# Swapping PSUM bank pairs, reordering steps and moving one input load in the prologue of a fused attention-and-MLP kernel

## The chip, the cores and the metric

The kernel runs on one core of one Trainium2 chip. The metric is the device time of one execution in microseconds (us); every run time quoted is a median of several executions. "Trace" and "profile" mean one execution recorded by the hardware profiler; a time inside an execution comes from one trace. Kernels are compared only within the same rounds.

## The reference, cut to what matters

```python
xn = layernorm(x)                                   # x: 2048 tokens x 448, in 16 tiles of 128 tokens
out = x + A(xn) + B(xn)
# A: linear attention, 16 heads of 28; q and k go through w_phi, then softmax(+) and softmax(-)
qkv = xn @ wqkv
phi_k = concat(softmax(k @ w_phi), softmax(-k @ w_phi));  kv = phi_k^T v;  ... ;  o @ wo
# B: mixer MLP
h  = gelu(layernorm(xn) @ w1);  h = shift_tokens(h) @ w2;  x1 = xn + h
     x1 + gelu(layernorm(x1) @ w3) @ w4
```

This is about the first 32 us. In that prologue the 16 tiles of x are loaded, normalised and transposed, V and the gelu of w1 are computed, and w_phi is folded into the q and k weights.

## The kernel before

PSUM, the memory that the matmuls here write their results to, is used as four pairs of banks, 0 to 3. To drain a pair is to copy its results out, which frees it for the next step. A step that goes to TensorE names its pair, and one instruction can drain both banks of a pair: V of tiles 2 and 3, 128x896, is drained by one ScalarE instruction of 0.91 us in the trace of this kernel. The program gives every engine its own list, and the traces show ScalarE's drains in the order of that list: tile 4's copy, V of tiles 2 and 3 and tile 5's copy, listed so, start at 12.07, 12.56 and 13.36 us here. A recorder derives the semaphore waits from which bytes and banks an instruction reads and writes, so choosing another pair changes who waits for whom without any other edit.

The names in the order list are these:

- `xn_T(i, b, n)` transposes n normalised tiles through pair b; ScalarE (or DVE) copies them to `xnT`.
- `V(i, k)` is half k of v for tiles i and i+1; `v_out(i, b)` drains it.
- `WA(g, k)` is w1's first two chunks of 128 columns for group g (four tiles), called "w1's first chunk" below; `wa_out` is its gelu.
- `WC(g, k)` is w1's third chunk for group g; `wc_out` is its gelu. `WD` is the fourth chunk.
- `spin(n, w)` issues n dummy matmuls that keep TensorE busy; `tables` is a table load on ScalarE (1.28 us in the trace).
- `FO(t, m, k)` folds w_phi into wk (t = 1) or wq (t = 0). DVE casts the results.

```python
load_x(0, 1)
load_x(1, 1, "ACT")
load_x(2, 1)
load_lap(wv, A_wqkv[:, 896:1344], ("ACT", "SP"))    # two halves of 224 KB, one on each queue
load_x(3, 1, "ACT")
load_x(4, 2)
...
def ln1_two(i):                                     # tiles 0,1 and 2,3
    for j in (i, i + 1):
        ln_stats(st, mv, xtok, j)                                        # DVE
        R.act(rs[:, j, 1:2], mv[:, j, 1:2], ACT.Sqrt, bias=epsb[:, 0:1]) # ScalarE
    for j in (i, i + 1):
        R.ew(dve, "reciprocal", rs[:, j, 0:1], rs[:, j, 1:2])
        ln1_apply(dve, j)
...
vps = {i: v_pair(i, b) for i, b in ((0, 2), (2, 3), (4, 1), (6, 3), (8, 1), (10, 1), (14, 3))}
was = {g: wa_pair(g, b) for g, b in ((0, 0), (1, 0), (2, 0), (3, 2))}
wcs = {g: wc_pair(g, b) for g, b in ((0, 2), (1, 2), (2, 0), (3, 3))}
...
play([(spin, 4, 256), V(0, 0), (xn_T, 2, 0), V(0, 1), (xn_T, 3, 1),
      (spin, 2, 256), V(2, 0), (v_out, 0, 2), (tables, "gelu_apprx_tanh_and_others"), WA(0, 0), (xn_T, 4, 1),
      V(2, 1), (v_out, 2, 3), (xn_T, 5, 2), WA(0, 1), WC(0, 0), (xn_T, 6, 3), WC(0, 1), (wc_out, 0, 2),
      V(4, 0), (xn_T, 7, 3), (wa_out, 0, 0), V(4, 1), (v_out, 4, 1), V(6, 0),
      ...
```

After the prologue come eight rounds of a k pair, a q pair and a side job, then the w3 and w4 stage to the end.

The softmax here doesn't subtract the row's maximum and nothing guards it: scores larger than these inputs give would overflow.

Of the kernel before, what the change touches and what calls it, by code (L numbers as in the profile page):

```python
# [5 lines left out]
ACT = mybir.ActivationFunctionType  # L6
# [214 lines left out]
def bass_parallel_sum__linear_kernel_hedgehog__mixer_s_mlp__prompt_kernel(  # L221
# [14 lines left out]
    with es:  # L236
# [18 lines left out]
        for b in range(4):  # L255
            t = es.enter_context(nc.psum_tensor("bank%d%d" % (2 * b, 2 * b + 1), [128, 1024], F32))
# [87 lines left out]
        def load_x(i, n, eng="SP"):  # L344
            R.dma(xtok[:, i:i + n, :], x2d[128 * i:128 * (i + n), :].rearrange("(j p) d -> p j d", p=128), eng)
# [5 lines left out]
        def load_lap(dst, src, engs=("SP", "SP")):  # L351
            for h in range(2):
                R.dma(dst[:, 2 * h:2 * h + 2, :], src[192 * h:192 * h + 256, :].rearrange("(c p) d -> p c d", p=128), engs[h])

        load_x(0, 1)
        load_x(1, 1, "ACT")
        load_x(2, 1)
        load_lap(wv, A_wqkv[:, 896:1344], ("ACT", "SP"))
        load_x(3, 1, "ACT")
        load_x(4, 2)  # L360
        load_x(6, 2)
        load_lap(w1, B_w1)
# [102 lines left out]
        def fold_pair(t, m, b):  # L465
            def side(k, hi):
                r, c0, c1 = (slice(64, CR), 2 * DH, CR) if hi else (slice(0, 64), 0, 3 * DH)
                return [(banks[2 * b + k][:, CR * c + c0:CR * c + c1],
                         wT[r, t, c, START[m + k]:START[m + k] + 128], bd[r, CR * c + c0:CR * c + c1])
                        for c in range(NC)]  # L470

            def late():
                row_pairs(side(1, 0), side(0, 1))
                if t:
                    R.ew(dve, "tensor_copy", wpk[:, m:m + 2, :], two(2 * b)[:, :, 0:D])
                    return
                for k in range(2):
                    a = banks[2 * b + k]
                    for j in range(2):
                        R.ew(dve, "tensor_copy",  # L480
                             wpq[:, m + k, :].rearrange("p (c j h e) -> p c j h e", c=NC, j=2, h=2)[:, :, j, :, 0:DH],
                             a[:, 224 * j:224 * j + 224].rearrange("p (c h e) -> p c h e", c=NC, h=2))
            return lambda: row_pairs(side(0, 0), side(1, 1), True), late
# [26 lines left out]
        def two(b):  # L510
            return pairs[b // 2].rearrange("p (b e) -> p b e", b=2)
# [3 lines left out]
        def row_pairs(first, second, start=False, cols=1):  # L515
            for s, (p, q) in enumerate(zip(first, second)):
                for out, lhs, rhs in (p, q) if cols == 1 else (*p, *q):
                    R.mm(out, lhs, rhs, start and s == 0, False)

        def lap_pair(outs, lhs, rhs):  # L520
            def side(k, rows, kcs):
                return [(outs[k], lhs(k, kc, *rows), rhs(k, kc, *rows)) for kc in kcs]
            return (lambda: row_pairs(side(0, LO, (0, 1, 2, 3)), side(1, HI, (0, 1, 2, 3)), True),
                    lambda: row_pairs(side(1, LO, (0, 1, 3)), side(0, HI, (0, 2, 3))))
# [11 lines left out]
        def v_pair(i, b):  # L536
            return lap_pair([banks[2 * b + k][:, 0:D] for k in range(2)],
                            lambda k, kc, lo, hi: xnT[lo:hi, kc, 128 * (i + k):128 * (i + k) + 128],
                            lambda k, kc, lo, hi: wv[lo:hi, kc, :])
# [9 lines left out]
        def wa_pair(g, b):  # L549
            return lap_pair([banks[2 * b + k] for k in range(2)],  # L550
                            lambda k, kc, lo, hi: w1[lo:hi, kc, 128 * k:128 * k + 128],
                            lambda k, kc, lo, hi: xnT[lo:hi, kc, 512 * g:512 * g + 512])
# [4 lines left out]
        def wc_pair(g, b):  # L557
            return lap_pair([banks[2 * b + k][:, 0:256] for k in range(2)],
                            lambda k, kc, lo, hi: w1[lo:hi, kc, 256:384],
                            lambda k, kc, lo, hi: xnT[lo:hi, kc, 512 * g + 256 * k:512 * g + 256 * k + 256])  # L560
# [4 lines left out]
        def wd_pair(h, b):  # L565
            def side(k, q, rows, kcs):
                lo, hi = rows
                t0 = 512 * (2 * h + q) + 256 * k
                return [(banks[2 * b + k][64 * q:64 * q + 64, 0:256], w1[lo:hi, kc, 384:448], xnT[lo:hi, kc, t0:t0 + 256])
                        for kc in kcs]  # L570
            up, down = (0, 1, 2, 3), ((0, 1, 3), (0, 2, 3))
            return (lambda: row_pairs([*zip(side(0, 0, LO, up), side(0, 1, LO, up))],
                                      [*zip(side(1, 0, HI, up), side(1, 1, HI, up))], True, 2),
                    lambda: row_pairs([*zip(side(1, 0, LO, down[0]), side(1, 1, LO, down[0]))],
                                      [*zip(side(0, 0, HI, down[1]), side(0, 1, HI, down[1]))], False, 2))
# [205 lines left out]
        def play(fs):  # L781
            for f in fs:
                f[0](*f[1:])
# [31 lines left out]
                xn_Td(i)  # L815
            late_3()

        vps = {i: v_pair(i, b) for i, b in ((0, 2), (2, 3), (4, 1), (6, 3), (8, 1), (10, 1), (14, 3))}
        was = {g: wa_pair(g, b) for g, b in ((0, 0), (1, 0), (2, 0), (3, 2))}
        wcs = {g: wc_pair(g, b) for g, b in ((0, 2), (1, 2), (2, 0), (3, 3))}  # L820
        wds = {h: wd_pair(h, b) for h, b in ((0, 1), (1, 0))}
        fps = {(t, m): fold_pair(t, m, b) for t, m, b in ((1, 0, 3), (1, 2, 2), (0, 0, 2), (0, 2, 3))}

        def V(i, k):
            return (vps[i][k],)

        def WA(g, k):
            return (was[g][k],)

        def WC(g, k):  # L830
            return (wcs[g][k],)

        def WD(h, k):
            return (wds[h][k],)

        def FO(t, m, k):
            return (fps[t, m][k],)

        play([(spin, 4, 256), V(0, 0), (xn_T, 2, 0), V(0, 1), (xn_T, 3, 1),
              (spin, 2, 256), V(2, 0), (v_out, 0, 2), (tables, "gelu_apprx_tanh_and_others"), WA(0, 0), (xn_T, 4, 1),  # L840
              V(2, 1), (v_out, 2, 3), (xn_T, 5, 2), WA(0, 1), WC(0, 0), (xn_T, 6, 3), WC(0, 1), (wc_out, 0, 2),
              V(4, 0), (xn_T, 7, 3), (wa_out, 0, 0), V(4, 1), (v_out, 4, 1), V(6, 0),
              WC(1, 0), V(6, 1), (v_out, 6, 3), WA(1, 0), WC(1, 1), (xn_T, 8, 1, 2), (wc_out, 1, 2), WA(1, 1), (wa_out, 1, 0),
              (xn_T, 10, 3, 2, "DVE"), (ln1_end,), V(8, 0), FO(1, 0, 0), V(8, 1), (v_out, 8, 1),
              WA(2, 0), FO(1, 0, 1), FO(1, 2, 0), WA(2, 1), (wa_out, 2, 0), FO(1, 2, 1),
              V(10, 0), (xn_T, 14, 3, 2), V(10, 1), (v_out, 10, 1), FO(0, 0, 0), WC(2, 0), FO(0, 0, 1), FO(0, 2, 0),
              WC(2, 1), (wc_out, 2, 0), FO(0, 2, 1), WD(0, 0), WD(1, 0), WD(0, 1), (wd_out, 0, 1), WD(1, 1), (wd_out, 1, 0),
              WA(3, 0), WC(3, 0), WA(3, 1), (wa_out, 3, 2), WC(3, 1), (wc_out, 3, 3)])
        for h in range(2):
            hop_out(h)  # L850
            hop_in(h)
# [12 lines left out]
        for ps in range(8):  # L864
            k, q = k_pair(2 * ps, 1), q_pair(ps // 2, 2 * (ps % 2), 0)
            w = (w2_pair if ps else v_pair)(side[ps], 2)
            if not ps:
                play([(k[0],), (q[0],), (k[1],), (k_exp, 0, 1, 0), (k_exp, 0, 1, 1), (w[0],), (q[1],), (q_exp, 0, 0, 0),
                      (q_exp, 0, 0, 1), V(14, 0), (w[1],), (v_out, 12, 2, "DVE"), V(14, 1), (v_out, 14, 3), (k_norm, 0)])
                continue  # L870
            k[0]()
            if ps > 2:
                kv_tile(2 * ps - 6)
                kv_tile(2 * ps - 5)
            w[0]()
            k[1]()
            for s in range(2):
                k_exp(2 * ps, 1, s)
            q[0]()
            w[1]()  # L880
            w2_out(side[ps], 2)
            q[1]()
            for s in range(2):
                q_exp(2 * ps, 0, s)
            if ps in (3, 5):
                ln_scale(mv2, rs2, ps - 3, 2, 2)
                for i in (ps - 3, ps - 2):
                    g_apply(i)
                    g_T(i)
            if ps == 7:  # L890
                ln_scale(mv2, rs2, 4, 2, 0)
            k_norm(2 * ps)
            for i in ((), (0,), (1,), (2,), (3,), (4,), (5,), (6, 7))[ps]:
                ln_stats(st2, mv2, xn, i)
# [90 lines left out]
```

## Time and profile before

| | before |
|---|---|
| time, median | 176.36 us (176.19 to 176.65, 3 runs) |
| span of the traced run | 174.7 us |
| TensorE busy | 169.2 us, 97% |
| first k matmul's weights | 32.02 us |

The first lines come from the page of the kernel before: the span, the busy time by engine, and the chain of waits by engine.

```profile
span 174.7 us, 5180 instructions
PE 169.2 (97%) x2254; PEld 90.8 (52%) x2254; DVE 114.5 (66%) x263; ACT 84.3 (48%) x99; POOL 88.7 (51%) x123
...
PE 90%; ACT 3%; DMA 3%; DVE 1%; ACTq 0%; issue 0%; DVEq 0%
```

The change takes no work from TensorE, so what it can gain is looked for in the 10% of the chain that are not TensorE. The next lines are pieces of that chain in order of time: start, length, and what it went through.

```profile
1.74 5.18 DMA xtok<-in_A_x_dram
...
9.35 0.60 ACT xnT L208
9.95 0.81 ACT vaug L208
...
10.77 1.28 ACT L386
...
12.07 0.60 ACT xnT L208
12.66 0.81 ACT vaug L208
13.47 0.50 ACT xnT L208
...
14.02 0.61 PE bank L200 x8
...
20.16 1.09 ACT xnT L208 x2
...
27.99 55.17 PE bank L200 x822
...
83.23 88.72 PE bank L200 x1060
```

The chain has one DMA (the load of x3, the fourth tile), then from 9.35 to 13.97 us ScalarE's drains and one table load (L386), at 20.16 two more ScalarE copies (tiles 8 and 9, for which V of 8/9 waits), and from 28 us on TensorE alone but for the very end. Two lines show the first and the last of these waits, DVE's for x3 and TensorE's at V of 8/9:

```profile
6.94 0.63 DVE L212 BATCH_NORM_STATS2 st<-xtok 128x6 f32<-128x448 bf16 x1 [0.28 <-DMA xtok<-in_A_x_dram]
...
21.30 0.49 PEld L200 LDWEIGHTS bank<-wv,xnT 64*128 64x128 bf16 x8 [0.42 <-ACT xnT L208]
```

The timeline of TensorE's weight loads (PEld) around 14 us shows what ScalarE's drains mean for TensorE. The bracket gives the idle time before the line and what ended it.

```profile
12.41 0.34 PEld L200 LDWEIGHTS bank<-xnT,w 64*128 64x128 bf16 x4
14.01 0.33 PEld L200 LDWEIGHTS bank<-xnT,w 64*128 64x128 bf16 x8 [1.27 <-ACT xnT L208]
14.36 0.27 PEld L204 LDWEIGHTS bank<-ident,xn 64*128 64x128 bf16 x8
```

The line at 14.01 is the third chunk of group 0. It reads tiles 0 to 3, which had been copied long before. What it waited for is its bank pair 2, which still held tile 5's transposes. ScalarE's timeline shows the drains:

```profile
12.07 0.60 ACT L208 ACTIVATE xnT<-bank 128x512 bf16<-128x512 bf16 x1
12.56 0.91 ACT L208 ACTIVATE vaug<-bank 128x896 bf16<-128x896 f32 x1
13.36 0.60 ACT L208 ACTIVATE xnT<-bank 128x512 bf16<-128x512 bf16 x1
```

They are tile 4's copy (pair 1), V of tiles 2 and 3 (pair 3), and tile 5's copy (pair 2). Pair 1 was free at 12.67, pair 2 only at 13.96.

### The profile page before, as it was taken

What the parts mean: (1) busy time and instruction counts of PE and PEld (TensorE: products, weight loads), DVE (VectorE), ACT (ScalarE), POOL (GpSimd) and SP (SyncE); (2) the same over time, 40 slices, a digit from 0 to 9 for tenths busy, and PEclk for the clock granted to TensorE, in tenths of its full rate; (3) what the DMA queues carried; (4) which work ended last, traced back from release to release, by engine and by line L of the source; (5) the groups of instructions that cost most, each with busy time, mean ns of one, the idle gap of its engine ahead of it and who ended that gap; (6) DMA issues with size and microseconds to landing.
All of it is one profiled execution on the core that took longest, in us unless ns stands there. A gap on an engine that the chain in (4) does not pass through costs nothing.

```text
span 174.7 us, 5180 instructions
## 1 busy us (share of the span) xinstructions
PE 169.2 (97%) x2254; PEld 90.8 (52%) x2254; DVE 114.5 (66%) x263; ACT 84.3 (48%) x99; POOL 88.7 (51%) x123
## 2 busy tenths in 40 slices
PE   7998999999999999999999999999999999999993
PEld 5454577544555555554555555545545555545451
DVE  4899896149999999985786972545427425474621
ACT  3497867697877777956224422223214222224000
POOL 3056570005879999950549389450720714523740
PEclk9999999999999999999999999999999999999999
DMA  5996541128961102034012842034411220313331
GB/s 162 341 215 81 124 100 41 38 49 271 389 239 35 30 8 56 4 33 91 5 29 60 71 85 61 25 86 90 94 30 53 62 56 4 83 30 34 83 102 33
DMA packets 32678, 15.20 MB, mean 87 GB/s; under 512 B 24080, under 2 KB 32016, under 8 KB 32656
## 3 DMA queue, kind: packets, MB, share of 16 engines
q1 hardware_dynamic: 31952, 14.36, 35.1%
q10 hardware_dynamic: 704, 0.52, 0.9%
q8 instruction: 17, 0.28, 0.7%
q14 instruction: 5, 0.04, 0.1%
HBM read 7.14 MB, written 1.84 MB: 51 GB/s over the span
## 4 chain that ended last, share of the span: by engine, by line
PE 90%; ACT 3%; DMA 3%; DVE 1%; ACTq 0%; issue 0%; DVEq 0%
PE bank L200 90%; DMA xtok<-in_A_x_dram 3%; ACT xnT L208 2%; ACT vaug L208 1%; ACT L386 1%; PE bank L204 1%; ACTq L218 0%; DVE st L212 0%; DVE xn L212 0%; DVE vaug L212 0%; DVEq L173 0%; DVE mv L212 0%; DVE rs L212 0%
## 5 line engine op out<-in xcount | busy, mean ns | idle before, releaser
L208 ACT ACTIVATE phik<-bank 128x1024 bf16<-128x1024 f32 (+1 forms) x44 | 42.3, 984 | 61.2 <-PE bank L200 61.2
L200 PE MATMUL bank<-gT,w 64*128 64x512 bf16 x392 | 50.2, 377 | 0.1
L212 DVE TENSOR_TENSOR vaug<-bank,vaug 128x464 f32<-128x464 f32 (+3 forms) x65 | 32.6, 512 | 23.0 <-PE bank L200 21.3
L200 PE MATMUL bank<-w,phik 64*128 64x448 bf16 (+1 forms) x420 | 45.0, 349 | 0.0
L212 POOL TENSOR_TENSOR xnT<-vaug 128x196 bf16<-128x196 f32 (+1 forms) x32 | 18.1, 586 | 46.6 <-DVE vaug L212 46.6
L200 PEld LDWEIGHTS bank<-w,phik 64*128 64x128 bf16 (+1 forms) x420 | 22.1, 94 | 20.8 <-issue 0.4
L212 POOL TENSOR_TENSOR phik<-phik,rks 128x1792 bf16<-128x1792 bf16 x8 | 25.6, 3215 | 10.4 <-DVE rks L212 10.3
L200 PEld LDWEIGHTS bank<-gT,w 64*128 64x128 bf16 x392 | 17.7, 94 | 17.6 <-issue 0.5
L212 POOL TENSOR_TENSOR vaug<-xn,xtok 128x448 f32<-128x448 bf16 x16 | 16.2, 1034 | 0.2 <-DVE vaug L212 0.2
L212 DVE TENSOR_REDUCE ksum<-phik 128x64 f32<-128x1792 bf16 x8 | 16.1, 2010 | 0.0
L212 DVE RECIPROCAL vaug<-bank 128x16 f32<-128x16 f32 x16 | 4.1, 257 | 18.2 <-PE bank L200 18.2
L200 PE MATMUL bank<-xnT,wpq 64*128 64x512 bf16 x112 | 14.7, 376 | 0.0
L200 PE MATMUL bank<-xnT,w 64*128 64x512 bf16 (+2 forms) x168 | 13.4, 306 | 0.8 <-ACT xnT L208 0.8
L200 PE MATMUL bank<-wv,xnT 64*128 64x448 bf16 x112 | 13.7, 351 | 0.4 <-ACT xnT L208 0.3
L200 PE MATMUL bank<-wo,xnT 64*128 64x448 bf16 (+1 forms) x106 | 13.4, 349 | 0.0
L200 PE MATMUL bank<-w,hT 64*128 64x448 bf16 x112 | 13.2, 349 | 0.0
L200 PE MATMUL bank<-wpk,xnT 64*128 64x448 bf16 x112 | 13.2, 349 | 0.0
L212 POOL TENSOR_TENSOR rs<-mv,mhalf 128x1 f32<-128x1 f32 (+2 forms) x16 | 10.8, 675 | 1.3
L212 DVE TENSOR_TENSOR xn<-bank,xn 128x512 bf16<-128x512 f32 (+1 forms) x16 | 9.2, 620 | 1.8 <-PE bank L200 1.8
L212 POOL TENSOR_SCALAR mv<-mv 128x1 f32<-128x1 f32 (+2 forms) x16 | 3.8, 238 | 12.5 <-DVE mv L212 12.0
L212 DVE BATCH_NORM_STATS2 st<-xtok 128x6 f32<-128x448 bf16 x16 | 9.8, 614 | 0.3 <-DMA xtok<-in_A_x_dram 0.3
L200 PEld LDWEIGHTS bank<-xnT,w 64*128 64x128 bf16 (+1 forms) x168 | 6.9, 98 | 4.6 <-ACT xnT L208 1.3
(67 smaller groups left out, 176.2 us busy)
## 6 DMA issues: line engine op xcount, KB each, us to landing
w<-in_B_w_dram SPq DMA_DIRECT2D x2, 896.0 KB, 6.0
out_dram<-vaug SPq DMA_DIRECT2D x15, 112.0 KB, 1.9
w<-in_B_w_dram SPq DMA_DIRECT2D x1, 1568.0 KB, 11.2
xtok<-in_A_x_dram SPq DMA_DIRECT2D x2, 448.0 KB, 6.5
xtok<-in_A_x_dram SPq DMA_DIRECT2D x2, 224.0 KB, 5.4
w<-in_B_w_dram SPq DMA_DIRECT2D x2, 224.0 KB, 5.6
wo<-in_A_wo_dram SPq DMA_DIRECT2D x2, 224.0 KB, 7.2
w<-in_B_w_dram SPq DMA_DIRECT2D x1, 336.0 KB, 3.6
```

Source lines behind the costliest of these rows:

```text
L200: self.op("PE", lambda e: e.matmul(out, lhsT, rhs, start=start, stop=stop, skip_group_check=True), [out], [lhsT, rhs], tile=self._tile(lhsT))
L204: self.op("PE", lambda e: e.transpose(out, in_, ident), [out], [in_, ident], tile=self._tile(in_))
L208: self.op("ACT", lambda e: e.activation(out, in_, func, **kw), [out], [in_] + aps)
L212: self.op(eng, lambda e: getattr(e, name)(out, *args, **kw), [out], aps)
L386: R.op("ACT", lambda e: e.preload_act_table_set(name), [], [])
```

## The change

The intent is to give the third chunk of groups 0 and 1, and V of tiles 4/5, 8/9 and 10/11, pairs that are already drained; to put the transposes of tiles 8 and 9 ahead of half a chunk; and to get x3 earlier. The third chunk of group 3 then falls on pair 0, so the first k/q round takes a new order in which q comes later. No instruction is added or removed.

```diff
--- before.py
+++ after.py
@@ -355,8 +355,8 @@
         load_x(0, 1)
         load_x(1, 1, "ACT")
         load_x(2, 1)
+        load_x(3, 1)
         load_lap(wv, A_wqkv[:, 896:1344], ("ACT", "SP"))
-        load_x(3, 1, "ACT")
         load_x(4, 2)
         load_x(6, 2)
         load_lap(w1, B_w1)
@@ -815,11 +815,11 @@
                 xn_Td(i)
             late_3()
 
-        vps = {i: v_pair(i, b) for i, b in ((0, 2), (2, 3), (4, 1), (6, 3), (8, 1), (10, 1), (14, 3))}
-        was = {g: wa_pair(g, b) for g, b in ((0, 0), (1, 0), (2, 0), (3, 2))}
-        wcs = {g: wc_pair(g, b) for g, b in ((0, 2), (1, 2), (2, 0), (3, 3))}
-        wds = {h: wd_pair(h, b) for h, b in ((0, 1), (1, 0))}
-        fps = {(t, m): fold_pair(t, m, b) for t, m, b in ((1, 0, 3), (1, 2, 2), (0, 0, 2), (0, 2, 3))}
+        vps = {i: v_pair(i, b) for i, b in ((0, 2), (2, 3), (4, 2), (6, 3), (8, 2), (10, 2), (14, 3))}
+        was = {g: wa_pair(g, b) for g, b in ((0, 0), (1, 0), (2, 0), (3, 3))}
+        wcs = {g: wc_pair(g, b) for g, b in ((0, 1), (1, 1), (2, 0), (3, 0))}
+        wds = {h: wd_pair(h, b) for h, b in ((0, 2), (1, 0))}
+        fps = {(t, m): fold_pair(t, m, b) for t, m, b in ((1, 0, 1), (1, 2, 3), (0, 0, 3), (0, 2, 1))}
 
         def V(i, k):
             return (vps[i][k],)
@@ -838,14 +838,14 @@
 
         play([(spin, 4, 256), V(0, 0), (xn_T, 2, 0), V(0, 1), (xn_T, 3, 1),
               (spin, 2, 256), V(2, 0), (v_out, 0, 2), (tables, "gelu_apprx_tanh_and_others"), WA(0, 0), (xn_T, 4, 1),
-              V(2, 1), (v_out, 2, 3), (xn_T, 5, 2), WA(0, 1), WC(0, 0), (xn_T, 6, 3), WC(0, 1), (wc_out, 0, 2),
-              V(4, 0), (xn_T, 7, 3), (wa_out, 0, 0), V(4, 1), (v_out, 4, 1), V(6, 0),
-              WC(1, 0), V(6, 1), (v_out, 6, 3), WA(1, 0), WC(1, 1), (xn_T, 8, 1, 2), (wc_out, 1, 2), WA(1, 1), (wa_out, 1, 0),
-              (xn_T, 10, 3, 2, "DVE"), (ln1_end,), V(8, 0), FO(1, 0, 0), V(8, 1), (v_out, 8, 1),
+              V(2, 1), (v_out, 2, 3), (xn_T, 5, 2), WA(0, 1), WC(0, 0), (xn_T, 6, 3), WC(0, 1), (wc_out, 0, 1),
+              V(4, 0), (xn_T, 7, 3), (wa_out, 0, 0), V(4, 1), (v_out, 4, 2), V(6, 0),
+              WC(1, 0), V(6, 1), (v_out, 6, 3), WA(1, 0), (xn_T, 8, 2, 2), WC(1, 1), (wc_out, 1, 1), WA(1, 1), (wa_out, 1, 0),
+              (xn_T, 10, 3, 2, "DVE"), (ln1_end,), V(8, 0), FO(1, 0, 0), V(8, 1), (v_out, 8, 2),
               WA(2, 0), FO(1, 0, 1), FO(1, 2, 0), WA(2, 1), (wa_out, 2, 0), FO(1, 2, 1),
-              V(10, 0), (xn_T, 14, 3, 2), V(10, 1), (v_out, 10, 1), FO(0, 0, 0), WC(2, 0), FO(0, 0, 1), FO(0, 2, 0),
-              WC(2, 1), (wc_out, 2, 0), FO(0, 2, 1), WD(0, 0), WD(1, 0), WD(0, 1), (wd_out, 0, 1), WD(1, 1), (wd_out, 1, 0),
-              WA(3, 0), WC(3, 0), WA(3, 1), (wa_out, 3, 2), WC(3, 1), (wc_out, 3, 3)])
+              V(10, 0), (xn_T, 14, 1, 2), V(10, 1), (v_out, 10, 2), FO(0, 0, 0), WC(2, 0), FO(0, 0, 1), FO(0, 2, 0),
+              WC(2, 1), (wc_out, 2, 0), FO(0, 2, 1), WD(0, 0), WD(1, 0), WD(0, 1), (wd_out, 0, 2), WD(1, 1), (wd_out, 1, 0),
+              WA(3, 0), WC(3, 0), WA(3, 1), (wa_out, 3, 3), WC(3, 1), (wc_out, 3, 0)])
         for h in range(2):
             hop_out(h)
             hop_in(h)
@@ -865,8 +865,8 @@
             k, q = k_pair(2 * ps, 1), q_pair(ps // 2, 2 * (ps % 2), 0)
             w = (w2_pair if ps else v_pair)(side[ps], 2)
             if not ps:
-                play([(k[0],), (q[0],), (k[1],), (k_exp, 0, 1, 0), (k_exp, 0, 1, 1), (w[0],), (q[1],), (q_exp, 0, 0, 0),
-                      (q_exp, 0, 0, 1), V(14, 0), (w[1],), (v_out, 12, 2, "DVE"), V(14, 1), (v_out, 14, 3), (k_norm, 0)])
+                play([(k[0],), (w[0],), (k[1],), (k_exp, 0, 1, 0), (k_exp, 0, 1, 1), (q[0],), (w[1],), (v_out, 12, 2, "DVE"),
+                      V(14, 0), (q[1],), (q_exp, 0, 0, 0), (q_exp, 0, 0, 1), V(14, 1), (v_out, 14, 3), (k_norm, 0)])
                 continue
             k[0]()
             if ps > 2:
```

## The prediction

> **What bounds the kernel now.** The page gives TensorE 97% of a 174.7 us span; the chain of waits is 90% TensorE and from 28 us on TensorE without a gap. Before that it is not: in the chain's pieces, from 1.74 to 14.02 us, it runs through the fourth x tile's transfer (5.18 us), DVE's first normalisations and, from 9.35 to 13.97, ScalarE alone, draining PSUM without a pause (copies of 0.60 and 0.81 us, a table load of 1.28). The timeline shows TensorE's gaps (matmuls or weight loads) there: 0.70 us before tile 2's transposes (8.33), 0.34 at 10.00, 1.27 before w1's third chunk of group 0 (12.75 to 14.01), 0.44 at 16.76 (tile 7's copy), 0.42 at 21.30 (copies of tiles 8 and 9). The 1.27 us is no data wait: the chunk needs tiles 0 to 3, long copied. Its bank pair 2 still holds tile 5's transposes, drained at 13.97.
>
> **What the change moves.** No instruction is added or removed.
> 1. The third chunk of groups 0 and 1 goes to pair 1, which tile 4's copy drained at 12.67. It can follow w1's first chunk at about 13.05 instead of 14.02: 1.0 us. Tile 6's transposes then start near 13.5 instead of 14.6, and ScalarE's 0.82 us idle before that copy goes. [...]
> 2. V of 4/5, 8/9 and 10/11 goes to pair 2. Tiles 8/9's transposes precede the second half of the third chunk, so their copies precede its gelu; V of 8/9 waits 0.1 to 0.3 us less.
> 3. x3 leaves the ACT queue, where it sat behind half of wv. DVE waited 0.28 us for it (statistics at 6.94), and tile 2's apply is behind that in DVE's order. wv's second half may land a little later, but V's first half has about 0.3 us of slack. Gain at most 0.28 us.
> 4. After the prologue, V of 12/13 goes ahead of q's first half, which waits for pair 0. q's exponentials start some 0.6 us later relative to the stage; ScalarE's 0.74 us idle at 39.2 to 39.9 absorbs this. Net near zero.
>
> **What limits the gain.** The sum is about 1.4 us. DVE normalises a tile each 1.12 us without a break; its slack against TensorE (tiles 8/9 2.2 us, 10/11 1.0, 14/15 1.4) falls nearly to zero, as does that of wpk's casts (24.10, 2.09 us), on which the last transposes wait. So I expect 1.0 to 1.2 us at the first k matmul (32.13 now, near 31.0 after). What follows is bound by TensorE, so it carries to the end.
>
> **Predicted: 175.2 us**, 8 in 10 between 174.6 and 176.0; faster by over 2%: 0.01, within 2%: 0.98, slower: 0.01.
>
> **What would show it.** The third chunk starts within 0.3 us of the end of w1's first; V of 8/9 near 20.2 instead of 21.30; statistics of x3 near 6.66; first k matmul near 31.0; TensorE's busy time nearly unchanged; the length from first k matmul to the end the same within 0.3 us.
>
> **What would make it wrong.** wv's second half or w1 landing too late; DVE's casts or ScalarE's drains making a new bank wait at V of 10/11, the third chunk of group 3 or q's first half; ScalarE falling behind in the first two k/q rounds.

One sentence of step 1 is cut where marked: it gave a rule, not shown in this case, and no time of its own. The sum of about 1.4 us is made of the four steps' 1.0, 0.1 to 0.3, at most 0.28 and near zero, and 0.2 to 0.4 was taken off it for DVE.

## The result, and the profile after

The changed kernel took 174.78 us (174.63 to 175.19, 4 runs) against 176.38 us before (4 runs): a ratio of 0.9912, 95% interval 0.989 to 0.9934. That is 1.6 us, inside the stated range and in its better half. A ratio here is the mean time of one kernel's fast runs over that of the other's of the same rounds, so it is not quite the ratio of the medians quoted. A second set of rounds, run for a second trace, gave 0.9921 (0.99 to 0.9943): 174.83 us (6 runs) against 176.07. Its expectation was 0.991, x3 landed before 5.2 us, wv's second half before 6.5 and the first k matmul at 30.5 to 30.7; x3 landed at 4.86, wv's second half at 6.97, later than expected, and the first k matmul's weights came at 30.45.

The same lines of the page of the changed kernel:

```profile
span 173.0 us, 5182 instructions
PE 168.8 (98%) x2254; PEld 90.0 (52%) x2254; DVE 114.2 (66%) x263; ACT 84.3 (49%) x99; POOL 88.7 (51%) x123
...
PE 97%; DVE 0%; ACT 0%; issue 0%; DVEq 0%
```

The chain is 97% TensorE instead of 90%, and DMA and ScalarE have all but left it.

The pieces of its chain from 6 us on:

```profile
6.46 1.62 PE bank L200 x12
8.08 0.22 PE bank L204 x8
8.30 0.58 PE bank L200 x6
8.88 0.14 PE bank L204 x8
...
9.04 0.61 ACT xnT L208
...
9.69 1.63 PE bank L200 x15
...
24.40 145.81 PE bank L200 x1924
```

The DMA piece of 5.18 us and the 4.6 us of ScalarE have left the chain; one ScalarE copy of 0.61 us is left. TensorE's busy time hardly moved (169.2 to 168.8), so the gain is idle time taken out. The weight loads around the third chunk, in the changed kernel:

```profile
12.09 0.99 PEld L200 LDWEIGHTS bank<-xnT,w 64*128 64x128 bf16 x12
13.28 0.20 PEld L204 LDWEIGHTS bank<-ident,xn 64*128 64x128 bf16 x8 [0.19 <-issue]
```

The twelve loads from 12.09 are four of w1's first chunk and the eight of the third chunk in one unbroken run. Tile 6's transposes come at 13.28 instead of 14.36. The statistics of x3 and V of 8/9 no longer wait:

```profile
6.64 0.59 DVE L212 BATCH_NORM_STATS2 st<-xtok 128x6 f32<-128x448 bf16 x1
...
19.71 0.49 PEld L200 LDWEIGHTS bank<-wv,xnT 64*128 64x128 bf16 x8
```

To see where the lead arises, the table takes the start of TensorE's weight loads at four points of both traces, and of a second trace of each kernel. The four stretches add up to the span.

| stretch (us) | before | before, 2nd | changed | changed, 2nd |
|---|---|---|---|---|
| start to tile 2's transposes | 8.33 | 7.78 | 8.00 | 7.89 |
| from there to the first k matmul | 23.69 | 23.71 | 22.54 | 22.56 |
| from there to the third k/q round | 9.69 | 9.69 | 9.66 | 9.65 |
| from there to the end | 132.97 | 133.19 | 132.76 | 132.78 |

The second stretch repeats to 0.02 us and holds 1.15 us of the gain. The third is unchanged. The last differs by up to 0.4 us between traces and is not explained by anything below. The first stretch moves by half a microsecond between two traces of the same kernel, so what x3 is worth needs care.

### The profile page after: what moved, and what is told of

The parts are those of the page before. It is cut to its first block, busy times and chain, and to the rows that moved or that the text cites. A ratio compares the mean times of both kernels' runs of the same rounds, so it can differ in the third digit from the quotient of the medians.

```text
span 173.0 us, 5182 instructions
## 1 busy us (share of the span) xinstructions
PE 168.8 (98%) x2254; PEld 90.0 (52%) x2254; DVE 114.2 (66%) x263; ACT 84.3 (49%) x99; POOL 88.7 (51%) x123
## 4 chain that ended last, share of the span: by engine, by line
PE 97%; DVE 0%; ACT 0%; issue 0%; DVEq 0%
PE bank L200 96%; PE bank L204 1%; ACT xnT L208 0%; DVE vaug L212 0%; DVEq L173 0%; DVE gT L212 0%
## 5 line engine op out<-in xcount | busy, mean ns | idle before, releaser
L212 DVE BATCH_NORM_STATS2 st<-xn 128x6 f32<-128x448 bf16 x16 | 9.2, 577 | 0.0
```

The source lines that it names most:

```text
L212: self.op(eng, lambda e: getattr(e, name)(out, *args, **kw), [out], aps)
```

## The experiments

My theory was that three independent parts add up: the bank swap (largest), the order of tiles 8/9's transposes (about 0.3 us), and x3 (about 0.3 us), while the new k/q order gains nothing itself and only pays for the third chunk's place on pair 0. The rivals were that DVE's pace of 1.12 us a tile (statistics at 13.04 and 14.16 in the kernel before) caps the gain, or that the parts overlap. Each time below is compared with the kernel before run in the same rounds (176.57, 176.07 and 176.30 us in the three sets). Six runs of each edited kernel, eleven of the kernel before. Stretches are as in the table above; "second stretch" is tile 2's transposes to first k matmul.

### x3 alone

```diff
 # kernel before
+        load_x(3, 1)
         load_lap(wv, A_wqkv[:, 896:1344], ("ACT", "SP"))
-        load_x(3, 1, "ACT")
```

> The kernel before with the x3 load alone moved to the SP queue behind x2; the banks as before. Theory (the gains add, because ScalarE's chain from 8.7 us only starts earlier and the wait for bank pair 2 shifts with it): tile 2's transposes at 8.00 to 8.05 us instead of 8.33, the third chunk at 13.7 instead of 14.02, first k matmul near 31.7 instead of 32.02, the whole 0.2 to 0.35 us faster than before (0.998). Rival (x3's time is slack that a later wait swallows): tile 2 earlier, but the third chunk still at 14.0 and the whole within 0.1 us of before.

Measured: 176.02 us against 176.57, ratio 0.9968 (0.9948 to 0.9987). Tile 2's transposes came at 7.90, the third chunk at 13.60 and the first k matmul at 31.60 instead of 32.02. The wait before the third chunk was 1.27 us as before, and so was the second stretch, 23.70 us. So what was won before tile 2 went through to the end (span 174.3 us against 174.7); it was not slack. The interval of the ratio is wide, 0.2 to 0.9 us, and does not fix the size better than the trace does.

### Banks and order alone

```diff
 # changed kernel
-        load_x(3, 1)
         load_lap(wv, A_wqkv[:, 896:1344], ("ACT", "SP"))
+        load_x(3, 1, "ACT")
```

> The changed kernel with the x3 load put back behind half of wv on the ACT queue; all bank and order changes kept. Theory (banks are the large part, parts add): tile 2's transposes back at 8.3, tile 6's transposes at 13.6 instead of 14.36 before, first k matmul near 30.85, the whole 1.2 to 1.35 us faster than before (0.993). Rival (the parts overlap: DVE's normalisation pace caps the gain at about 1.2 us whatever x3 does): first k matmul within 0.1 us of the changed kernel's 30.54.

Measured: 175.25 us, ratio 0.9923 (0.9901 to 0.9945). The second stretch was 22.55 us, within 0.01 of the changed kernel's. First k matmul at 31.01, not at the 30.54 that the rival foresaw. The start of this trace was late (8.46 at tile 2's transposes) for two reasons: x3 landed at 6.87 and DVE waited 0.22 us for it, and the dummy matmuls were slow (three took 0.82 us instead of 0.50), as shown under the DVE run below. So it is the equal second stretch, more than the 31.01, that speaks against the rival: what is won after tile 2 is the same with x3 early or late.

### Tiles 8 and 9 late again

```diff
 # changed kernel
-  WA(1, 0), (xn_T, 8, 2, 2), WC(1, 1), (wc_out, 1, 1), WA(1, 1)
+  WA(1, 0), WC(1, 1), (xn_T, 8, 2, 2), (wc_out, 1, 1), WA(1, 1)
```

> The changed kernel with the transposes of tiles 8 and 9 put back behind the second half of w1's third chunk of group 1 (they stay on pair 2). Theory (the step from 1.27 us of lead at tiles 10/11's transposes to 1.59 at V of 8/9 comes from the copies of tiles 8/9 starting a third-chunk half earlier): V of 8/9 at about 20.0 instead of 19.71, with a wait of about 0.3 us for those copies, and 0.2 to 0.35 us slower than the changed kernel, so 1.25 to 1.4 faster than before (0.9925). Rival (the lead there comes from pair 2 being free, not from the order): V of 8/9 at 19.7 and no loss.

Measured: 175.26 us, ratio 0.994 (0.9908 to 0.9971), which overlaps the changed kernel's. The trace decides: V of 8/9 at 20.13 instead of 19.71, and a second stretch of 22.84 instead of 22.54. The wait that the kernel before had at 21.30 is back, shown in the weight loads of this run:

```profile
19.22 0.49 PEld L204 LDWEIGHTS bank<-ident,xn 64*128 64x128 bf16 x16
20.13 0.49 PEld L200 LDWEIGHTS bank<-wv,xnT 64*128 64x128 bf16 x8 [0.42 <-ACT xnT L208]
```

In the changed kernel V of 8/9 has no wait there. The order is worth 0.3 us. This run holds all the bank changes without that order, and its 22.84 against 23.70 puts them together at about 0.85 of the 1.15 us. No run changed one bank pair alone, so what each is worth is not shown.

### The first k/q round in its old order

```diff
 # changed kernel
-  play([(k[0],), (w[0],), (k[1],), (k_exp, ...), (k_exp, ...), (q[0],), (w[1],), (v_out, 12, 2, "DVE"),
-        V(14, 0), (q[1],), (q_exp, ...), (q_exp, ...), V(14, 1), (v_out, 14, 3), (k_norm, 0)])
+  play([(k[0],), (q[0],), (k[1],), (k_exp, ...), (k_exp, ...), (w[0],), (q[1],), (q_exp, ...),
+        (q_exp, ...), V(14, 0), (w[1],), (v_out, 12, 2, "DVE"), V(14, 1), (v_out, 14, 3), (k_norm, 0)])
```

> The changed kernel with the first k/q round put back in its old order (q's first half before V of 12/13). Theory (the new order is there only because q's bank pair 0 is now drained last, by the gelu of the third chunk of group 3, which ended at 32.05): q's first half waits about 0.7 us for ScalarE, its start at 32.1 instead of the 31.4 that the k half leaves free; the q exponentials start without ScalarE's 0.69 us of idle; the second k/q round starts 0.3 to 0.7 us later than the changed kernel's 35.95, and the whole is 0.2 to 0.7 us slower than the changed kernel. Rival (ScalarE is what bounds the first two k/q rounds, so the order of TensorE's work before it does not matter): the third round (40.20) and the whole unchanged within 0.1 us.

Measured: 175.58 us, ratio 0.9949 (0.9926 to 0.9971). The second stretch stayed at 22.56 and the third grew from 9.66 to 10.39 us. The weight loads of this run show the wait for pair 0:

```profile
30.73 0.58 PEld L200 LDWEIGHTS bank<-wpk,xnT 64*128 64x128 bf16 x8
32.28 0.55 PEld L200 LDWEIGHTS bank<-xnT,wpq 64*128 64x128 bf16 x8 [0.96 <-ACT hT L208]
```

The second round began 0.7 us later relative to the first k matmul, and the third too, so ScalarE does not absorb it and the rival falls; the loss is at the upper end of what my theory gave. The new order keeps 0.73 us that the third chunk's move to pair 0 would otherwise cost.

### The third chunk of group 3 on pair 2, and the old k/q order

```diff
 # changed kernel, with the old k/q order of the last run
-  wcs = {... (2, 0), (3, 0)}        (wc_out, 3, 0)
+  wcs = {... (2, 0), (3, 2)}        (wc_out, 3, 2)
```

> The changed kernel with the third chunk of group 3 on pair 2 instead of pair 0, and with the first k/q round in its old order (q's first half second), as pair 0 is then free early. Theory (the changed kernel loses 0.1 to 0.4 us of its lead of 1.59 us at that chunk, whose weights wait 0.38 us for the second of the two gelus of the fourth chunk; pair 2 is drained by the first of them, about 0.5 us earlier; and the old order costs time only where q must wait for pair 0): no wait of 0.38 us there, first k matmul near 30.3, q's first half without a wait, the whole 0.1 to 0.4 us faster than the changed kernel. Rival (the old order of the k/q round costs by itself what the run with only the order put back lost, 0.7 us): slower than the changed kernel by 0.3 us or more although the first k matmul is earlier.

Measured: 175.00 us, ratio 0.9937 (0.991 to 0.9964), which is the changed kernel's within the noise. The second stretch was 22.49 and the third 9.69 us. The old order costs nothing once pair 0 is free, so the rival falls. But the whole was not faster, and my theory's own number was wrong too: the wait of 0.38 us is gone and the first k matmul gained only 0.05. The changed kernel's weight loads had it:

```profile
28.30 0.55 PEld L200 LDWEIGHTS bank<-xnT,w 64*128 64x128 bf16 x8 [0.20 <-issue]
29.23 1.31 PEld L200 LDWEIGHTS bank<-xnT,w 64*128 64x128 bf16 x20 [0.38 <-ACT hT L208]
30.54 0.58 PEld L200 LDWEIGHTS bank<-wpk,xnT 64*128 64x128 bf16 x8
```

and this run's do not:

```profile
28.30 2.17 PEld L200 LDWEIGHTS bank<-xnT,w 64*128 64x128 bf16 x28 [0.20 <-issue]
30.49 0.58 PEld L200 LDWEIGHTS bank<-wpk,xnT 64*128 64x128 bf16 x8
```

In both traces the 84 matmuls of the stretch before the first k matmul form one group without a recorded break, 4.42 us from 26.39 in the changed kernel and 4.35 us from 26.41 in this run, and all the weight loads above start within it. So the weights were loaded while matmuls ran, and with the 0.38 us pause of the weight loader removed only 0.05 us was gained.

### ScalarE's table load taken out, before and after

```diff
 # kernel before, and the same edit on the changed kernel
-  tables("sqrt_and_others")
+  tables("gelu_apprx_tanh_and_others")
 # ln1_two: tiles 0 to 3 scaled on GpSimd like the others
-  R.act(rs[:, j, 1:2], mv[:, j, 1:2], ACT.Sqrt, ...);  R.ew(dve, "reciprocal", ...)
+  ln1_stats(j, 1, 0)
-  (v_out, 0, 2), (tables, "gelu_apprx_tanh_and_others"), WA(0, 0)
+  (v_out, 0, 2), WA(0, 0)
```

> The kernel before, banks and loads untouched, with ScalarE's table load of 1.28 us taken out of the drain chain: tiles 0 to 3 get their scale on GpSimd like all others, so no square root on ScalarE and the gelu table is loaded once at the start. Theory (the 1.27 us before the third chunk is pair 2 waiting for ScalarE's queue of drains): the chunk starts 0.5 to 1.0 us earlier than 14.01 and its wait shrinks to 0.2 to 0.7 us, although tile 3 is normalised some 0.3 us later; the whole 0.3 to 0.9 us faster than before. Rival (the wait is set by data or by DVE's normalisation of tile 5, not by ScalarE): the chunk at 14.0 or later.

> The same removal of the table load in the changed kernel. Theory (after the bank change ScalarE's queue is no longer what TensorE waits for, but DVE's normalisation pace of 1.12 us a tile, which becomes 0.3 us later at tile 3): within 0.3 us of the changed kernel, either sign; V of tiles 6/7 at 15.2 to 15.6 (15.49 in the changed kernel). Rival (ScalarE still bounds the prologue): V of 6/7 at 14.9 or earlier and the whole 0.5 us or more faster than the changed kernel.

Both theories missed. The kernel before got slower, 177.06 us, ratio 1.0043 (1.0019 to 1.0068). The changed kernel with the same edit took 175.84 us, ratio 0.9979 (0.996 to 0.9998): 1 us slower than without the edit, with a second stretch of 22.91 instead of 22.54. The second stretches of the two edited kernels, 23.87 and 22.91 us, differ by 0.96, so without the table load the change still keeps most of its 1.15. The path through GpSimd delays the first tiles: tile 3's transposes came at 9.57 us in the edited kernel before instead of 8.85, and the third chunk at 14.53. ScalarE, in the edited kernel before, is no longer busy without a pause:

```profile
12.51 0.60 ACT L208 ACTIVATE xnT<-bank 128x512 bf16<-128x512 bf16 x1 [1.19 <-PE bank L204]
...
13.08 0.92 ACT L208 ACTIVATE vaug<-bank 128x896 bf16<-128x896 f32 x1
...
13.89 0.59 ACT L208 ACTIVATE xnT<-bank 128x512 bf16<-128x512 bf16 x1
...
14.53 0.33 PEld L200 LDWEIGHTS bank<-xnT,w 64*128 64x128 bf16 x8 [1.23 <-ACT xnT L208]
```

It idles 1.19 us before tile 4, and the third chunk still waits 1.23 us. So "ScalarE is saturated" is not the reason for that wait, and the rival, which said data or normalisation, has the later start right (14.53) but not the wait. What is common to both traces is the order: V's drain stands between tile 4's copy and tile 5's copy. The next run tests that.

### Only ScalarE's order, in the kernel before

```diff
 # kernel before
-  V(2, 1), (v_out, 2, 3), (xn_T, 5, 2), WA(0, 1)
+  V(2, 1), (xn_T, 5, 2), (v_out, 2, 3), WA(0, 1)
```

> The kernel before with one change on ScalarE: tile 5's copy (pair 2) comes before the drain of V of tiles 2/3 (pair 3), banks and loads as before. Theory (the 1.27 us before the third chunk is the drain of pair 2 standing behind that V drain in ScalarE's order; taking the table load away did not help since ScalarE then waited for tile 4 instead): the chunk starts at 13.2 to 13.3 us instead of 14.01; but tile 6's transposes then wait for the V drain of pair 3, so they start near 14.0 instead of 14.36, and only 0.3 to 0.4 us of the 0.8 is kept: V of 4/5 at 14.5 to 14.6, the whole 0.2 to 0.4 us faster than before. Rival (the chunk waits for something else than pair 2's drain): chunk at 14.0, whole unchanged.

Measured: 175.69 us against 176.30, ratio 0.9963 (0.9938 to 0.9988). In this trace x3 happened to land early, so the second stretch is the fair measure: 23.31 us against 23.71 and 23.69, a gain of 0.4. The third chunk came 4.97 us after tile 2's transposes against 5.68 and 5.70 in the two traces of the kernel before, 0.7 us earlier. The weight loads of this run:

```profile
12.89 0.33 PEld L200 LDWEIGHTS bank<-xnT,w 64*128 64x128 bf16 x8 [0.53 <-ACT xnT L208]
13.76 0.20 PEld L204 LDWEIGHTS bank<-ident,xn 64*128 64x128 bf16 x8 [0.54 <-DVE mv L212]
```

The wait for pair 2 shrank from 1.27 to 0.53 us, and a new one of 0.54 us stands before tile 6's transposes. The label there names a DVE statistic, but tile 6's pair 3 is the one that V's drain, now later, has just left (it ran from 12.74 to 13.65); tile 6 itself had been normalised at 12.70. So the chunk waits for a bank whose drain stands behind another drain in ScalarE's list. Reordering the drains moved part of the wait to another bank. Giving the chunk a free bank removed it: in the changed kernel its loads follow w1's first chunk in one run from 12.09.

### DVE relieved by one instruction

```diff
 # changed kernel
-  phi_blocks()                       # 0.38 us on DVE, before tile 9
   ...
   ln1_apply(dve, 11)
+  phi_blocks()
```

> The changed kernel with the one DVE instruction of 0.38 us that builds the block matrix moved behind the normalisation of tile 11. Theory (after the change DVE's pace touches TensorE only in short weight-load gaps of 0.17 to 0.36 us at the casts, which the array hides): first k matmul within 0.15 us of the changed kernel's 30.5, the whole the same within 0.15 us. Rival (as the prediction had it: DVE's pace caps the gain): tile 8/9's and 10/11's transposes and the first k matmul 0.2 to 0.4 us earlier, the whole 0.2 to 0.4 us faster than the changed kernel.

Measured: 175.18 us, ratio 0.9928 (0.9908 to 0.9949). The second stretch was 22.54 us, exactly the changed kernel's. DVE's pace up to tile 11 caps nothing. The run does not reach the later casts of wpk, which started 14.76 us after tile 2's transposes here and 14.77 in the changed kernel.

In this trace everything before 8.5 us was late, as in the run with the banks alone and in both runs without the table load. The matmuls of this run show why. The group with gT is a run of dummy matmuls that keep TensorE busy:

```profile
5.78 0.82 PE L200 MATMUL bank<-gT 128*128 128x256 bf16 x3
...
6.86 0.61 PE L200 MATMUL bank<-gT 128*128 128x256 bf16 x4
7.40 1.15 PE L200 MATMUL bank<-wv,xnT 64*128 64x448 bf16 x8
```

and the same stretch of the changed kernel's first trace:

```profile
5.73 0.50 PE L200 MATMUL bank<-gT 128*128 128x256 bf16 x3
...
6.39 0.61 PE L200 MATMUL bank<-gT 128*128 128x256 bf16 x4
6.93 1.15 PE L200 MATMUL bank<-wv,xnT 64*128 64x448 bf16 x8
```

Three dummy matmuls took 0.82 us instead of 0.50, and V started 0.47 us later. In every trace the dummy matmuls start at 1.25 or 1.26 us and follow each other every 0.21 us, and later every 0.11 us; the pace doubled about 3.3 us after the first of them in the run with x3 alone and about 5.7 us after it in the run with the banks alone. Of all fourteen traces, the three dummy matmuls took 0.82 us in four, 0.59 in one and 0.50 or 0.51 in nine, in kernels with different edits. The profile's granted clock does not show the change of pace (1.00 from 5.5 to 7.5 us in both traces above). What sets the moment at which the pace doubles is not shown. In the traces shown the start is about 0.45 us later with the slow pace, which is another reason to compare from tile 2's transposes on.

### x3 on the ACT queue, but first

```diff
 # changed kernel
-        load_x(3, 1)
+        load_x(3, 1, "ACT")
         load_lap(wv, A_wqkv[:, 896:1344], ("ACT", "SP"))
```

> The changed kernel with x3 on the ACT queue again, but ahead of the first half of wv there. Theory (x3 was late because 224 KB of wv stood before it in its queue, whichever queue that is): x3 lands before 5.2 us as in the changed kernel (4.8 to 5.1), statistics of x3 without a wait at 6.5 to 6.7, tile 2's transposes at 7.9 to 8.1, the whole as the changed kernel within 0.2 us. Rival (the queue matters, not the order): x3 lands after 6 us and 0.3 us is lost.

Measured: 175.39 us, ratio 0.9941 (0.9917 to 0.9964). x3 landed at 4.08 us, on the queue on which it landed at 5.73 to 6.92 behind wv's first half, so here the place in the queue decided and not the queue. But wv's first half, now last on that queue, landed at 7.17 instead of 4.50, and V waited for it: it started at 7.27 instead of 6.93 or 6.84. The second stretch was 22.75: this order of the queue gives 0.2 us back of the change's gain.

### The kernel before once more

```diff
 # kernel before, no edit
```

> The kernel before unaltered, for a second trace. In four traces with x3 behind half of wv it landed at 6.92, 6.87, 6.42 and 5.98 us, and only the first two made DVE wait. If that spread is the order's and not the edits', this trace has x3 between 5.9 and 7.0, tile 2's transposes between 7.9 and 8.4 and the first k matmul between 31.6 and 32.1; the third chunk follows w1's first by the same wait of 1.2 to 1.3 us as before.

Measured: x3 landed at 5.73 us, earlier than the stated 5.9, so DVE did not wait for it and tile 2's transposes came at 7.78 and the first k matmul at 31.49, both also just below their ranges. The wait before the third chunk was 1.27 us again. In the five traces with x3 behind half of wv it landed at 6.92, 6.87, 6.42, 5.98 and 5.73 us, and only the first two made DVE wait. In the eight with x3 ahead of wv's second half on the SP queue it landed between 4.79 and 5.37. So x3's 112 KB landed later behind 224 KB of wv, in every trace, than ahead of wv's second half. What spreads the two traces of the same program by 1.2 us (6.92 and 5.73) is not shown. Of the four later traces with the old order, the late one is from chip 7 and the three early ones are from chips 2, 3 and 6. Whether the spread is one of runs or of chips is not shown.

## Why the prediction was right or wrong

- **What bounds the prologue.** Right. The third chunk's 1.27 us was a bank wait. The prediction's wording that ScalarE drained "without a pause" was true of the trace but was not the cause; with the table load gone and ScalarE idle for 1.19 us the wait was still 1.23. It was the place of the drain in ScalarE's list.
- **Step 1, the bank swap, 1.0 us.** The runs show about 0.85 us for all bank changes together (second stretch 22.84 against 23.70). Counted from tile 2's transposes, the changed kernel's trace was ahead by 0.75 us at tile 6's transposes and by 0.94 at V of 6/7.
- **Step 2, tiles 8/9 first, 0.1 to 0.3 us.** Right at its upper end: undoing it cost 0.30 us.
- **Step 3, x3, at most 0.28 us.** In the two traces compared it was 0.33 us. The fear that wv's second half would land later did not show: 7.09 before, 6.40 after, and 6.08 to 6.97 in the other traces with this order, against 5.96 to 7.09 with the old one. The prediction took one trace's landing of x3 for a fixed quantity. It is not: in three of five traces of the old order x3 came in time. How often x3 was late in the timed runs behind the 1.6 us is not recorded, so that this part of the number came out is in part luck. Its average worth is left open: 0.3 to 0.4 us in the traces where x3 was late, nothing where it came in time, and 0.2 to 0.9 us by the timed run of this step alone.
- **Step 4, the k/q order, near zero.** Right against the kernel before (9.69 and 9.66 us). Undone, it costs 0.73 us, so it is a needed part of the swap and not a gain.
- **"What limits the gain".** This is the term that was mis-sized. The prediction had a sum of 1.4 us and took off 0.2 to 0.4 because DVE's slack and the casts of wpk would run out. Call "lead" how much earlier a step came than in the kernel before. DVE's slack did run out: its idle of 0.73 us before the copies of tiles 10 and 11 (at 21.05 in the kernel before) was gone, and weight loads of the changed kernel waited 0.17, 0.18 and 0.36 us for DVE, the last two for those casts. But TensorE lost nothing by it: it was busy for 8.00 of the 8.00 us from 22 to 30 in the changed kernel, and the lead was 1.59 us at V of 8/9 and still 1.59 at the fourth chunk (27.98 before, 26.39 after). Relieving DVE of 0.38 us moved nothing. DVE's idle had been a wait for TensorE (the profile names TensorE's transposes as what ended it), so its later work moved forward with TensorE: the casts started at 22.77 instead of 24.10. Slack read from one trace, as a distance between two engines of which one follows the other, was not a fixed limit here. The lead at the first k matmul was 1.48 us, the three parts measured above (0.85, 0.30 and 0.33). The 0.11 us went after the casts, at the last chunks, where the weight loads waited 0.23 and 0.38 us for ScalarE's gelus (0.17 and nothing in the kernel before); the run with pair 2 got 0.05 of it back.
- **The signs to look for.** Statistics of x3 at 6.64 (6.66 foretold), the third chunk without a gap behind w1's first, V of 8/9 at 19.71 (20.2 foretold), first k matmul at 30.65 with its weights at 30.54 (31.0 foretold), TensorE's busy time 0.4 us less. The two misses are the same one: the prediction took off for DVE what TensorE did not lose.
- **"What follows is bound by TensorE, so it carries to the end."** Right. From the first k matmul to the end it took 142.66 us before and 142.42 after.

No run beat the changed kernel. The variant with pair 2 and the old k/q order equals it.

## What to carry to other kernels

When an engine waits for a bank, ask which drain holds that bank and how many drains stand ahead of it in that engine's list; here a bank whose drain was already over removed a wait of 1.27 us, while reordering the drains left 0.53 us of it and put 0.54 us before the next bank's transposes. The delays before tile 2's transposes, be it a load or a trip through another engine, reached the end in these runs (span 174.3 us with x3 early alone and 175.1 with the trip through GpSimd, against 174.7 before; second stretches 23.70, 23.87 and 23.69), while a start of V that was 0.4 us later (x3 first on the ACT queue) cost 0.2; so try a load that a first tile needs ahead of bulk weights, and check in the trace that it does not push the weights behind the point where they are needed. When the effect is below half a microsecond, compare a stretch that starts after the noisy beginning (two traces of the kernel before gave 8.33 and 7.78 us up to tile 2's transposes, and 23.69 and 23.71 from there to the first k matmul), and take two traces of the same kernel before believing a wait in one.
